# A planner that knows VectorE's pause behind a result it needs: delta-rule attention and a SwiGLU layer on one core

## The chip, the core and the metric

The kernel runs on one core of a Trainium2 chip. A core has five engines that run side by side, each through its own list of instructions in order: TensorE (PE) multiplies matrices, VectorE (DVE) and ScalarE (ACT) do elementwise work, GpSimd (POOL) does small odd jobs, and SyncE (SP) issues most DMA transfers. The metric is the device time of one execution in microseconds (us), the median of several runs.

## The reference

There are two layers in a row. The first is DeltaNet attention over 4 batches and 8 heads with 768 steps and head size 48:

```python
for t in range(S):
    kt, vt, bt = (k_n[:, :, t], v[:, :, t], beta[:, :, t, None])
    y[:, :, t] = np.einsum('bhd,bhde->bhe', q[:, :, t], state)
    v_old = np.einsum('bhde,bhd->bhe', state, kt)
    state = state + bt[:, :, :, None] * np.einsum('bhd,bhe->bhde', kt, vt - v_old)
```

Here `k_n` is `k` divided by its norm. The result, 3072 tokens of width 384, goes through an RMS norm with gain and a SwiGLU layer of width 1536: `(silu(xn @ w_gate) * (xn @ w_val)) @ w_out`. All inputs arrive in 64-bit or 32-bit floats as the reference makes them; the kernel computes in fp32.

## The kernel before

**Tiles.** The 768 steps are cut into 12 tiles (`c` from 0 to 11) of 64 steps. Inside a tile the step-by-step recurrence becomes matrix algebra. A triangular matrix of key products is inverted, and that inverse times a right-hand side gives the tile's updates `u_`. The `state` goes from tile to tile. Each tile's outputs then go through the SwiGLU layer (`ffn_plain` for tiles 0 and 1, `ffn` for tiles 2 to 11).

**The inverse.** Tiles 0 and 1 invert blocks of 16 (`prep16`), tiles 2 to 11 blocks of 32 (`invert`). The work is a chain on VectorE. After a few opening operations (L1023, L1048, L1053, L1058) come 15 steps, 7 in `prep16`. Each step is a `tensor_tensor` that multiplies into the scratch `acc` (L1070; L903 in `prep16`) and a `tensor_reduce` that adds three planes of it (L1076; L909). Each of these reads what the one in front of it wrote. Behind the last step the inverse is copied out, written to DRAM (`dx`, `dxt`) and read back by DMA in other layouts (`m1bd`, `x2bd`, `mt`). TensorE then merges it (L1124, L1152) and multiplies it with the right-hand side (L1281). After that `u_` (L1349, L1351) leads to `pu` (L1317), `ku` (L1404) and the new state.

**Weights.** The SwiGLU weights arrive as 64-bit floats in 18 pieces of 768 columns. `weights` converts each with one ScalarE operation (L619) and VectorE operations L607, L610 and L615. The last sum of the two halves is done in one of two ways: on TensorE by two products with the identity into PSUM and a ScalarE copy (L631, L632, L636) for pieces `n < NPE`, or on VectorE (L639) for the others. `NPE` is 1, so piece 0 takes the first way.

**The SwiGLU layer.** `ffn_plain` makes its products at L1558 and L1540. Before tile 2's layer, VectorE forms sums of the weights (`factors`, L1616; `out_factors`, L1687). `ffn` then uses them for a fast scheme with fewer products: for each of two halves 15 products (L1651), whose results are added up on VectorE (L1661) or copied by ScalarE (L1663), and then `down` (L1708, L1717).

**The planner.** No order of instructions is written out. Each piece of work is put into a `Plan` with `P.add(engine, duration, function, priority, r=reads, w=writes)`. One such operation may issue one or several instructions. `Plan.forward` lays the operations out in time with the given durations: of all operations that are ready, the one that can start first goes next, and the key decides between equals. On VectorE an operation may start `OVERLAP["DVE"]` = 0.08 us before the one ahead of it ends, and before the change this holds also for one that needs the other's result. `Plan.backward` turns a finished layout into new keys. `run` does that for a number of rounds, then tries the shakes of keys whose seeds stand in `MOVES`, each from where the last left off, and keeps the best order. That order is what each engine gets. Before time 70 `filler` puts spare products (L1826) where the layout leaves TensorE empty.

The diff touches `Plan.add`, `forward` and `backward`, the two `step` functions of `prep16` and `invert`, `NPE`, and the durations that several `P.add` calls are given.

Of the kernel before, what the change touches and what calls it, by code (L numbers as in the profile page):

```python
# [20 lines left out]
L = 16  # L21
# [4 lines left out]
ROUNDS, MOVES = (22, 17), (22002180, 22002182, 22003335, 22003342, 22003359, 22003366, 22003748, 22003755, 22003872, 22003889, 22003903, 22003920, 22003934, 22003951, 22003980, 22004653, 22004660, 22004729, 22004746, 22004753, 22004770, 22004784, 22004801, 22004870, 22004877, 22004894, 22004901, 22004918, 22004925, 22004932, 22004949, 22004994, 22005011, 22005221, 22008697, 22008780, 22010194, 22010220, 22010239, 22010256, 22010270, 22010287, 22010301, 22010318, 22010400, 22010466, 22010535, 22010559, 22010560, 22010566, 22010583, 22010590, 22010614, 22010676, 22010683, 22010700, 22010707, 22010714, 22010731, 22010738, 22013940, 22014280, 22014565, 22014620, 22014780, 22014860, 22015546, 22015640, 22016400, 22016640, 22019860, 22020512, 22020620, 22020980, 22021900, 22022178, 22022500, 22023240, 22023744, 22024759, 22025599, 22028580, 22432695, 22434395, 22436663, 22437300, 22438400, 22439440, 22441380, 22441780, 22442460, 22442900, 22730144, 22731520, 22731920, 22731968, 22731982, 22732667, 22734384, 22734484, 22734852, 22735265, 22735300, 22735678, 22736628, 22736790, 22736838, 22737523, 22737533, 22737829, 22738662, 22738951, 22740560, 22746034, 22747420, 22747741, 22748419, 22749152, 22749290, 22753826, 22754194, 22755471, 22755620, 22756220, 22756789, 22757140, 22758049, 22758160, 22759790, 22760680, 22762300, 22763820, 22766102, 22766200, 22767004, 22767644, 22767940, 22768119, 22769086, 22771213, 22773629, 22773808, 22776028, 22785537, 22851960, 22853134, 22856837, 22860912, 22861215, 22862065, 22863655, 22864481, 22865240, 22865320, 22866860, 22869820, 22898160, 22899809, 22901540, 22901620, 22902120, 22902927, 22906589, 22906700, 22907300, 22907540, 22908258, 22910819, 22910877, 22911445, 22912860, 22913386, 22918927, 22919082, 22919880, 22920476, 22922892, 22922909, 22923180, 22923960, 22924706, 22926702, 22926967, 22928120, 22928416, 22928557, 22929276, 22929700, 22938627, 22940028, 22940145, 22940630, 22942998, 22943731, 22944000, 22944137, 22944285, 22944574, 22944715, 22945414, 22946570, 22947417, 22947699, 22948384, 22948477, 22950700, 22951100, 22952944, 22955921, 22956334, 22957415, 22967671, 22968620, 23135508, 23135773, 23136045, 23136069, 23136100, 23136186, 23137876, 23138585, 23139731, 23139865, 23140612, 23140877, 23142006, 23142520, 23143245, 23144220, 23144460, 23144640, 23145389, 23146680, 23149200, 23149620, 23149700, 23149932, 23151911, 23153000, 23153329, 23155077, 23155490, 23157118, 23160928, 23161513, 23163940, 23166040, 23172120, 23180693, 23181278, 23181371, 23181691, 23181722, 23182283, 23182383, 23182407, 23182782, 23182803, 23183216, 23183388, 23183512, 23183653, 23183694, 23183949, 23184090, 23184107, 23186217, 23186499, 23186967, 23187091, 23188237, 23188502, 23191307, 23191751, 23194752, 23194814, 23196170, 23233009)  # L26
# [8 lines left out]
SHAKE = 0.12  # L35
SPARE = 0.5
# [35 lines left out]
class Plan:  # L72
# [48 lines left out]
    def forward(self, banks, until):  # L121
# [43 lines left out]
        while len(order) < len(self.ops):  # L165
# [78 lines left out]
    def backward(self):  # L244
# [8 lines left out]
        while left:  # L253
# [91 lines left out]
def kernel(  # L345
# [57 lines left out]
    NPE, NRAW, NCV = 1, 3, 2  # L403
# [94 lines left out]
    def setup():  # L498
# [12 lines left out]
        P.add("POOL", 1.0, lambda: make_identity(nc, ident), 0, w=["ident"])  # L511
# [22 lines left out]
        P.add("DVE", 0.9, places2, 2, r=["ident"], w=["put"])  # L534
        P.add("ACT", 1.7, lambda: nc.scalar.activation(out=rs[0], in_=mhalf, func=ACTF.Silu), -1, r=["half"], w=[("rs", 0)])
# [34 lines left out]
    def weights(n0, n1):  # L570
# [14 lines left out]
        for n, (dst, src, keys) in list(enumerate(todo))[n0:n1]:  # L585
# [33 lines left out]
            P.add("ACT", 0.84, lambda high=high, top=top: nc.scalar.activation(out=top, in_=high.bitcast(FP32), func=ACTF.Prelu, scale=2.0**-112, alpha=2.0**32), pr, r=rk, w=cak)  # L619
# [163 lines left out]
    def prep16(c):  # L783
# [113 lines left out]
        for j in range(0, L - 2, 2):  # L897
            n, m = j + 2, L - 2 - j

            def step(j=j, n=n, m=m):  # L900
# [7 lines left out]
                )  # L908
                nc.vector.tensor_reduce(  # L909
# [6 lines left out]
            P.add("DVE", 0.37 + 0.0052 * n * m, step, pi, r=ab, w=ak)  # L916
# [93 lines left out]
    def invert(c):  # L1010
# [28 lines left out]
        P.add("ACT", 0.5, start, pd, r=["half"], w=AK)  # L1039
        P.add("ACT", 0.9, start2, pd + 0.5, r=bkeys, w=AK)  # L1040
# [22 lines left out]
        P.add("DVE", 0.3, share3, pi, r=[("at", 0), ("at", 1)], w=AK)  # L1063
        P.add("DVE", 0.69, share2, pi, r=xkeys, w=[("at", 0), ("at", 1)])
        for j in range(0, W - 2, 2):
            n, m = j // 2 + 1, W - 2 - j

            def step(j=j, n=n, m=m):
# [6 lines left out]
                )  # L1075
                nc.vector.tensor_reduce(  # L1076
# [6 lines left out]
            P.add("DVE", 0.37 + 0.0052 * n * m, step, pi, r=[("at", 0), ("at", 1)], w=AK)  # L1083
# [93 lines left out]
    def recur(c):  # L1177
# [175 lines left out]
        def change(h):  # L1353
            for g_, xs in places(h):
                P.add("DVE", V(384), lambda xs=xs, g_=g_: nc.vector.tensor_tensor(out=parts(zb, h, xs), in0=found(g_), in1=parts(u_, h, xs), op=ALU.subtract), pr, r=[g_, *uk(h)], w=zk(h))
# [67 lines left out]
        for h in halves:  # L1423
# [13 lines left out]
            else:  # L1437
                for g in range(2):
# [3 lines left out]
                    ), py, r=[gy[g]], w=[("yn", p) for p in range(2)])  # L1442
                for p in range(2):

                    P.add("ACT", A(384) + 0.2, lambda p=p, gy=gy: nc.scalar.activation(
                        out=gy[p].t[:, 0:DM], in_=yn[:, p], func=ACTF.Square, scale=1.0 / math.sqrt(DM), accum_out=ms[i2][:, p, 0:1],
                    ), py, r=[("yn", p)], w=[gy[p], ("ms", i2, p)], last=gy[p])
# [9 lines left out]
            P.add("POOL", 1.1 if c else 0.7, root, py, r=["half"], w=[(k_, i2, p) for p in h for k_ in ("ms", "rs")])  # L1457
# [5 lines left out]
            else:  # L1463
                for p in range(2):
                    P.add("ACT", A(384), lambda p=p: nc.scalar.mul(yn[:, p], yn[:, p], rs[i2][:, p : p + 1]), py, r=[("rs", i2, p)], w=[("yn", p)])
            if c >= XSQ:
# [7 lines left out]
                for k_ in range(KT):  # L1474
                    P.add("ACT", A(256), lambda k_=k_: nc.scalar.mul(xf[:, 2 * k_ : 2 * k_ + 2], xf[:, 2 * k_ : 2 * k_ + 2], g_sb[:, k_ : k_ + 1]), pxv, r=["g"], w=[xkeys[0]] + ([xkeys[1]] if k_ == KT - 1 else []))  # L1475
                continue
            for p in h:
# [16 lines left out]
                for k_ in range(KT):  # L1494
                    P.add("ACT", A(128), lambda p=p, psx=psx, k_=k_: nc.scalar.mul(
                        xdst[:, 2 * k_ + p], psx.t[:, 128 * k_ : 128 * k_ + 128], g_sb[:, k_ : k_ + 1]
                    ), pxv, r=[psx, "g"], w=[xkeys[p]], last=psx)
        if c > 1:
            X = lambda a, n, step=1: xf[:, a : a + step * (n - 1) + 1 : step]
            for dst, a, b_, op, n in (  # L1500
# [11 lines left out]
                ), pxv, r=[("xp", 0)], w=["xc", ("xp", 1), ("cva", 0)])  # L1512
# [349 lines left out]
```

## Time and profile before

| what | us |
|---|---|
| median of 3 runs | 671.26 (670.19 to 671.73) |
| the profiled execution | 677.52 |
| its span, first to last instruction | 675.8 |
| TensorE busy | 657.2 (97%) |
| VectorE busy | 576.2 (85%) |
| ScalarE busy | 297.9 (44%) |
| GpSimd busy | 88.0 (13%) |

The profiled execution took 6.26 us more than the median of the runs. The profile's groups name the source line, the engine, the operation and its tiles, then the number of instructions, their busy time, the mean duration of one in ns, and the idle time in front of them with what ended it. TensorE records an fp32 product twice. Ends of TensorE records are modelled, so its busy time says less about its real load than that of other engines. A timeline row gives start and duration in us.

### The profile page before, as it was taken

The numbers are of one execution on the slowest core, as the hardware profiler recorded it, in microseconds if no ns is written. First come the engines' busy times: TensorE is split into PE (matmuls) and PEld (weight loads), VectorE is DVE, ScalarE is ACT, GpSimd is POOL, SyncE is SP. The second block draws the span as 40 slices with busy tenths as digits, with TensorE's granted clock in tenths as the row PEclk, the third lists the DMA queues.
The fourth block names the chain that finished last, engine by engine and source line by source line (L and its number), as shares of the span: only waits on it lengthen the run. The fifth ranks groups of instructions, "written<-read, shape, count | busy, mean of one in ns | idle before, by whom it ended". The sixth has DMA issues, their size and how long they took to land.

```text
span 675.8 us, 23477 instructions
## 1 busy us (share of the span) xinstructions
PE 657.2 (97%) x10052; PEld 607.2 (90%) x10052; DVE 576.2 (85%) x1200; ACT 297.9 (44%) x683; POOL 88.0 (13%) x105
## 2 busy tenths in 40 slices
PE   8898999999999999999899999999999999999997
PEld 6876777778799999999899999999999999999997
DVE  5998889999999998997899899899899699457473
ACT  7553543524336445345246336246345344343341
POOL 4113111031031030030030021030031001000000
PEclk9998999999999999999899999999999999999999
DMA  9574577636415457347447437457437434202100
GB/s 227 127 191 129 118 191 165 137 59 112 63 24 96 68 132 117 59 110 116 74 101 126 77 90 132 82 117 123 80 77 125 80 58 82 47 2 48 24 1 24
DMA packets 270430, 64.40 MB, mean 95 GB/s; under 512 B 256979, under 2 KB 262134, under 8 KB 270326
## 3 DMA queue, kind: packets, MB, share of 16 engines
q1 hardware_dynamic: 267046, 62.12, 46.5%
q8 instruction: 79, 1.29, 0.8%
q10 hardware_dynamic: 3280, 0.79, 0.6%
q14 instruction: 25, 0.20, 0.1%
HBM read 45.30 MB, written 17.56 MB: 93 GB/s over the span
## 4 chain that ended last, share of the span: by engine, by line
PE 65%; DVE 21%; SPq 5%; DMA 4%; issue 3%; ACT 1%; POOL 0%; DVEq 0%; POOLq 0%; ACTq 0%
PE bank L1651 35%; PE bank L1708 15%; SPq L487 5%; DVE acc L1076 4%; DVE acc L1070 3%; PE bank L1558 3%; PE bank L704 3%; PE bank L1199 2%; PE bank L1317 1%; DVE tmp L1661 1%; DMA at<-dkk 1%; PE bank L1540 1%; DVE more L1616 1%; DMA q<-in_q_dram 1%; DMA x2bd<-dx 1%
## 5 line engine op out<-in xcount | busy, mean ns | idle before, releaser
L1651 PE MATMUL bank<-xf,w_in 128*128 128x128 f32 x1440 | 179.2, 276 | 0.6 <-DVE tmp L1661 0.6
L1651 PEld LDWEIGHTS bank<-xf,w_in 128*128 128x128 f32 x1440 | 169.8, 192 | 1.7 <-DVE tmp L1661 0.8
L1661 DVE TENSOR_TENSOR tmp<-tmp,bank 128x512 f32<-128x512 f32 x180 | 119.8, 680 | 27.9 <-PE bank L1651 24.3
L1651 PE MATMUL bank<-xf,more 128*128 128x128 f32 x960 | 124.9, 277 | 1.8 <-DVE tmp L1661 1.8
L1651 PEld LDWEIGHTS bank<-xf,more 128*128 128x128 f32 x960 | 115.2, 192 | 4.3 <-DVE tmp L1661 3.2
L1663 ACT COPY tmp<-bank 128x512 f32<-128x512 f32 x120 | 68.1, 585 | 64.8 <-PE bank L1651 52.9
L1667 ACT ACTIVATE tmp<-tmp 128x256 f32<-128x256 f32 x120 | 49.7, 417 | 98.0 <-DVE tmp L1661 97.3
L731 POOL TENSOR_TENSOR knrm<-ksum,half 128x16 f32<-128x16 f32 x12 | 35.8, 2981 | 324.8 <-DVE ksum L730 309.5
L1076 DVE TENSOR_REDUCE acc<-acc 128x30 f32<-128x90 f32 (+4 forms) x150 | 70.9, 473 | 5.1
L1708 PE MATMUL bank<-wo_sb,hf 128*128 128x192 f32 x360 | 64.0, 328 | 0.0
L1708 PEld LDWEIGHTS bank<-wo_sb,hf 128*128 128x128 f32 x360 | 58.2, 191 | 0.7 <-ACT tmp L1713 0.2
L1070 DVE TENSOR_TENSOR acc<-acc,at 128x60 f32<-128x60 f32 (+4 forms) x150 | 52.7, 351 | 2.3
L1668 DVE TENSOR_TENSOR hf<-tmp 128x256 f32<-128x256 f32 x120 | 48.5, 420 | 6.6 <-ACT tmp L1667 5.5
L1540 PE MATMUL bank<-wo_sb,hf 128*128 128x384 f32 x96 | 35.3, 496 | 1.9 <-DVE hf L1566 1.8
L1558 PE MATMUL bank<-xf,w_in 128*128 128x256 f32 x144 | 34.8, 392 | 0.2 <-DVE hf L1566 0.2
L1558 PE MATMUL bank<-xp,w_in 128*128 128x256 f32 x144 | 33.8, 382 | 0.0
L1558 PEld LDWEIGHTS bank<-xp,w_in 128*128 128x128 f32 x144 | 26.8, 190 | 5.5 <-DVE hf L1566 0.3
L1558 PEld LDWEIGHTS bank<-xf,w_in 128*128 128x128 f32 x144 | 26.9, 192 | 4.7 <-DVE hf L1566 0.5
L1565 ACT ACTIVATE tmp<-bank 128x256 f32<-128x256 f32 x24 | 9.2, 383 | 43.7 <-PE bank L1558 36.4
L1713 ACT COPY tmp<-bank 128x192 f32<-128x192 f32 x30 | 9.5, 317 | 42.0 <-PE bank L1708 40.2
L1540 PEld LDWEIGHTS bank<-wo_sb,hf 128*128 128x128 f32 x96 | 17.3, 190 | 11.8 <-DVE hf L1566 3.7
L1510 DVE TENSOR_TENSOR xf<-xf 128x256 f32<-128x256 f32 (+1 forms) x70 | 24.0, 382 | 1.9 <-ACT xf L1475 1.1
(203 smaller groups left out, 988.6 us busy)
## 6 DMA issues: line engine op xcount, KB each, us to landing
at<-dkk SPq DMA_DIRECT2D x20, 256.0 KB, 3.8
more<-in_moe_w_gate_dram SPq DMA_DIRECT2D x6, 768.0 KB, 5.3
vt<-in_v_dram SPq DMA_DIRECT2D x24, 192.0 KB, 4.2
k<-in_k_dram SPq DMA_DIRECT2D x23, 192.0 KB, 4.3
out_dram<-tmp SPq DMA_DIRECT2D x46, 96.0 KB, 2.2
more<-in_moe_w_val_dram SPq DMA_DIRECT2D x5, 768.0 KB, 7.0
more<-in_moe_w_out_dram SPq DMA_DIRECT2D x5, 768.0 KB, 7.3
dsq<-k SPq DMA_DIRECT2D x6, 512.0 KB, 2.6
```

The costliest lines, as they stand in the source:

```text
L487: op = P.add(eng, dur + (0.08 if eng == "SP" else 0.0), lambda: queue.dma_start(out=dst, in_=src), prio, r, w, lat=0.7)
L731: P.add("POOL", 2.95, lambda: nc.gpsimd.tensor_tensor(out=knrm[i2], in0=ksum[i2], in1=half, op=ALU.pow), pn, r=[("ksum", i2), "half"], w=[ ...
L1070: nc.vector.tensor_tensor(out=acc[:, 1:3, 0:n, j + 2 : W].rearrange("p a i t -> p i a t"), in0=acc[:, old, 0:n, j : j + 2, None].to_broadc ...
L1076: nc.vector.tensor_reduce(out=acc[:, new, 0:n, j + 2 : W], in_=acc[:, lo : lo + 3, 0:n, j + 2 : W].rearrange("p a i t -> p i t a"), axis=A ...
L1540: nc.tensor.matmul(po[p].t[:, 0:DM], hf[:, spot(f), 128 * p : 128 * p + 128], wo_sb[:, spot(f)], start=(f == f0), stop=(f == f1 - 1), skip ...
L1558: nc.tensor.matmul(ps.t[:, TOK * side : TOK * side + TOK], w_in[:, side, h_, 3 * t + i_, n : n + 128], x_[:, 2 * t : 2 * t + 2].rearrange( ...
L1651: nc.tensor.matmul(g.t[:, 128 * z : 128 * z + 128], fac[:, side, 128 * f : 128 * f + 128], xf[:, xs], start=(begin and z == 0), stop=False ...
L1661: P.add("DVE", V(512), lambda t=t, g=g: nc.vector.tensor_tensor(out=t, in0=t, in1=g.t, op=ALU.add), -1, r=[g], w=[tk], last=g)
L1663: P.add("ACT", A(512), lambda t=t, g=g: nc.scalar.copy(t, g.t), -1, r=[g], w=[tk], last=g)
L1667: P.add("ACT", A(256), lambda t=t: nc.scalar.activation(out=t[:, 0:256], in_=t[:, 0:256], func=ACTF.Silu), -1, w=[tk])
L1668: P.add("DVE", V(256), lambda t=t, f0=f0, p=p: nc.vector.tensor_tensor(out=hf[:, spot(f0) : spot(f0) + 2, 128 * p : 128 * p + 128], in0=t[ ...
L1708: nc.tensor.matmul(g.t[:, 0:192], a_[:, f], b_[:, f], start=(begin and f == 0), stop=(f == 5), skip_group_check=True)
```

## The change

1. **The pause.** A constant `TIED = 0.034` is added. In `forward`, an operation that needs the result of a VectorE operation, itself on VectorE, may start only 0.034 us behind that one's end. Before, it could start 0.08 us ahead of the end. An operation with the new flag `loose=True` keeps the old rule. `backward` gets the same term. `loose` is set at four kinds of operations (L1058, L1355, L1439, L1510), which share a key with the one ahead without using its result.
2. **The steps.** Each inverse step, so far one operation of the plan with two instructions, becomes two operations, `spans` (the multiplication) and `sums_` (the reduction). The instructions themselves are the same.
3. **Durations.** The figures that the planner is given for a dozen operations are altered (identity, `places2`, the first activation, weight conversion on ScalarE, the clearing of `acc`, the square, the GpSimd root, the scaled copies).
4. **The first piece.** `NPE` goes from 1 to 0: the sum of weight piece 0 is done on VectorE (L639).
5. **The search.** `ROUNDS, MOVES` hold another seed, another number of rounds and another list: 278 seeds before, 282 after.

Since the planner works out the order anew, every engine's order differs.

```diff
-ROUNDS, MOVES = (22, 17), (
...
+ROUNDS, MOVES = (21, 13), (
...
+TIED = 0.034
...
-    def add(self, eng, dur, fn, prio, r=(), w=(), lat=0.15, ps=(), last=(), size=0):
+    def add(self, eng, dur, fn, prio, r=(), w=(), lat=0.15, ps=(), last=(), size=0, loose=False):
...
-        op.size, op.first = size, self.first
+        op.size, op.first, op.loose = size, self.first, loose
...
-                u.at = max(u.at, at[op.eng] if u.eng == op.eng and not op.dma else end + op.hop(u) + u.slack)
+                u.at = max(u.at, (end + TIED if op.eng == "DVE" and not u.loose else at[op.eng]) if u.eng == op.eng and not op.dma else end + op.hop(u) + u.slack)
...
-                gap = d.end - d.start - d.dur + (0.0 if d.eng == op.eng and not d.dma else d.hop(op) + op.slack)
+                gap = d.end - d.start - d.dur + ((TIED if d.eng == "DVE" and not op.loose else 0.0) if d.eng == op.eng and not d.dma else d.hop(op) + op.slack)
...
-    NPE, NRAW, NCV = 1, 3, 2
+    NPE, NRAW, NCV = 0, 3, 2
...
-        P.add("POOL", 1.0, lambda: make_identity(nc, ident), 0, w=["ident"])
+        P.add("POOL", 0.6, lambda: make_identity(nc, ident), 0, w=["ident"])
...
         for j in range(0, W - 2, 2):
             n, m = j // 2 + 1, W - 2 - j
 
-            def step(j=j, n=n, m=m):
+            def spans(j=j, n=n, m=m):
                 old, new, lo = (3, 0, 1) if j % 4 else (0, 3, 0)
                 nc.vector.tensor_tensor(
                     out=acc[:, 1:3, 0:n, j + 2 : W].rearrange("p a i t -> p i a t"),
...
                     op=ALU.mult,
                 )
+
+            def sums_(j=j, n=n, m=m):
+                old, new, lo = (3, 0, 1) if j % 4 else (0, 3, 0)
                 nc.vector.tensor_reduce(
                     out=acc[:, new, 0:n, j + 2 : W],
                     in_=acc[:, lo : lo + 3, 0:n, j + 2 : W].rearrange("p a i t -> p i t a"),
...
-            P.add("DVE", 0.37 + 0.0052 * n * m, step, pi, r=[("at", 0), ("at", 1)], w=AK)
+            P.add("DVE", 0.15 + 0.0021 * n * m, spans, pi, r=[("at", 0), ("at", 1)], w=AK)
+            P.add("DVE", 0.165 + 0.0034 * n * m, sums_, pi, r=[("at", 0), ("at", 1)], w=AK)
...
-        P.add("ACT", 0.5, start, pd, r=["half"], w=AK)
-        P.add("ACT", 0.9, start2, pd + 0.5, r=bkeys, w=AK)
+        P.add("ACT", 1.05, start, pd, r=["half"], w=AK)
+        P.add("ACT", 0.66, start2, pd + 0.5, r=bkeys, w=AK)
...
-        P.add("DVE", 0.3, share3, pi, r=[("at", 0), ("at", 1)], w=AK)
+        P.add("DVE", 0.3, share3, pi, r=[("at", 0), ("at", 1)], w=AK, loose=True)
...
-            P.add("POOL", 1.1 if c else 0.7, root, py, r=["half"], w=[(k_, i2, p) for p in h for k_ in ("ms", "rs")])
+            P.add("POOL", 1.1, root, py, r=["half"], w=[(k_, i2, p) for p in h for k_ in ("ms", "rs")])
...
-                    P.add("ACT", A(384), lambda p=p: nc.scalar.mul(yn[:, p], yn[:, p], rs[i2][:, p : p + 1]), py, r=[("rs", i2, p)], w=[("yn", p)])
+                    P.add("ACT", A(384) + 0.1, lambda p=p: nc.scalar.mul(yn[:, p], yn[:, p], rs[i2][:, p : p + 1]), py, r=[("rs", i2, p)], w=[("yn", p)])
```

The steps of `prep16` are split in the same way.

More of the change, by code (lines that the diff above doesn't have):

```diff
@@ L533, in setup @@
         P.add("DVE", 0.7, places, 1, r=["ident"], w=["pick"])
-        P.add("DVE", 0.9, places2, 2, r=["ident"], w=["put"])
-        P.add("ACT", 1.7, lambda: nc.scalar.activation(out=rs[0], in_=mhalf, func=ACTF.Silu), -1, r=["half"], w=[("rs", 0)])
+        P.add("DVE", 1.32, places2, 2, r=["ident"], w=["put"])
+        P.add("ACT", 0.25, lambda: nc.scalar.activation(out=rs[0], in_=mhalf, func=ACTF.Silu), -1, r=["half"], w=[("rs", 0)])
         P.add("POOL", 0.7, masks, 0, w=["mask"])
@@ L615, in s5 @@
                 nc.vector.scalar_tensor_tensor(out=cc, in0=low, scalar=by, in1=cc, op0=ALU.mult, op1=ALU.mult)
-            P.add("ACT", 0.84, lambda high=high, top=top: nc.scalar.activation(out=top, in_=high.bitcast(FP32), func=ACTF.Prelu, scale=2.0**-112, alpha=2.0**32), pr, r=rk, w=cak)
+            P.add("ACT", 0.92, lambda high=high, top=top: nc.scalar.activation(out=top, in_=high.bitcast(FP32), func=ACTF.Prelu, scale=2.0**-112, alpha=2.0**32), pr, r=rk, w=cak)
             P.add("DVE", 0.57, s2, pr, w=cak)
@@ L908, in step @@
                 )
+            def sums_(j=j, n=n, m=m):
+                old, new, lo = (3, 0, 1) if j % 4 else (0, 3, 0)
+                cols = slice(L * c + j + 2, L * c + L)
                 nc.vector.tensor_reduce(
@@ L914, in step @@
                 )
-            P.add("DVE", 0.37 + 0.0052 * n * m, step, pi, r=ab, w=ak)
+            P.add("DVE", 0.15 + 0.0021 * n * m, spans, pi, r=ab, w=ak)
+            P.add("DVE", 0.165 + 0.0034 * n * m, sums_, pi, r=ab, w=ak)
         xflat = x.rearrange("p i t -> p (i t)")
@@ L1066, in invert, with spans @@
             n, m = j // 2 + 1, W - 2 - j
-            def step(j=j, n=n, m=m):
+            def spans(j=j, n=n, m=m):
                 old, new, lo = (3, 0, 1) if j % 4 else (0, 3, 0)
@@ L1075, in step, with sums_ @@
                 )
+            def sums_(j=j, n=n, m=m):
+                old, new, lo = (3, 0, 1) if j % 4 else (0, 3, 0)
                 nc.vector.tensor_reduce(
@@ L1354, in change @@
             for g_, xs in places(h):
-                P.add("DVE", V(384), lambda xs=xs, g_=g_: nc.vector.tensor_tensor(out=parts(zb, h, xs), in0=found(g_), in1=parts(u_, h, xs), op=ALU.subtract), pr, r=[g_, *uk(h)], w=zk(h))
+                P.add("DVE", V(384), lambda xs=xs, g_=g_: nc.vector.tensor_tensor(out=parts(zb, h, xs), in0=found(g_), in1=parts(u_, h, xs), op=ALU.subtract), pr, r=[g_, *uk(h)], w=zk(h), loose=True)
         for h in halves:
@@ L1441, in recur @@
                         in1=gy[g].t[:, 0:DM].rearrange("s (y e) -> s y e", e=D), op=ALU.add,
-                    ), py, r=[gy[g]], w=[("yn", p) for p in range(2)])
+                    ), py, r=[gy[g]], w=[("yn", p) for p in range(2)], loose=True)
                 for p in range(2):
-                    P.add("ACT", A(384) + 0.2, lambda p=p, gy=gy: nc.scalar.activation(
+                    P.add("ACT", A(384), lambda p=p, gy=gy: nc.scalar.activation(
                         out=gy[p].t[:, 0:DM], in_=yn[:, p], func=ACTF.Square, scale=1.0 / math.sqrt(DM), accum_out=ms[i2][:, p, 0:1],
@@ L1474, in recur @@
                 for k_ in range(KT):
-                    P.add("ACT", A(256), lambda k_=k_: nc.scalar.mul(xf[:, 2 * k_ : 2 * k_ + 2], xf[:, 2 * k_ : 2 * k_ + 2], g_sb[:, k_ : k_ + 1]), pxv, r=["g"], w=[xkeys[0]] + ([xkeys[1]] if k_ == KT - 1 else []))
+                    P.add("ACT", A(256) + 0.09, lambda k_=k_: nc.scalar.mul(xf[:, 2 * k_ : 2 * k_ + 2], xf[:, 2 * k_ : 2 * k_ + 2], g_sb[:, k_ : k_ + 1]), pxv, r=["g"], w=[xkeys[0]] + ([xkeys[1]] if k_ == KT - 1 else []))
                 continue
@@ L1494, in recur @@
                 for k_ in range(KT):
-                    P.add("ACT", A(128), lambda p=p, psx=psx, k_=k_: nc.scalar.mul(
+                    P.add("ACT", A(128) + 0.07, lambda p=p, psx=psx, k_=k_: nc.scalar.mul(
                         xdst[:, 2 * k_ + p], psx.t[:, 128 * k_ : 128 * k_ + 128], g_sb[:, k_ : k_ + 1]
```

4 lines of the change are left out of this document (2 added, 2 removed).

## The prediction

> **What bounds the kernel now.** I read the page's totals first, then the busy time of each engine by stretch.
>
> ```profile
> span 675.8 us, 23477 instructions
> PE 657.2 (97%) x10052; PEld 607.2 (90%) x10052; DVE 576.2 (85%) x1200; ACT 297.9 (44%) x683; POOL 88.0 (13%) x105
> ```
>
> ```profile
> 0.00:20.00 20.00, 16.51 (x286) 12.45 (x286) 12.90 (x47) 14.06 (x24) 6.83 (x16) 1.00 0.86 199
> 20.00:240.00 220.00, 212.26 (x3418) 177.97 (x3419) 206.14 (x415) 98.41 (x223) 35.94 (x34) 0.99 0.54 115
> 240.00:500.00 260.00, 256.51 (x4252) 247.72 (x4252) 233.89 (x493) 116.84 (x279) 35.64 (x41) 0.99 0.55 100
> 500.00:600.00 100.00, 100.00 (x1479) 97.66 (x1479) 79.14 (x165) 43.40 (x103) 8.64 (x14) 1.00 0.40 73
> 600.00:675.80 75.80, 71.94 (x636) 71.41 (x628) 44.12 (x83) 25.19 (x58) 0.92 (x2) 1.00 0.09 22
> ```
>
> The columns after the stretch's length are PE, its weight loads, VectorE, ScalarE, GpSimd, granted clock, DMA share, GB/s. TensorE looks full everywhere, but its weight loads tell more: 97.66 of 100 us late in the run, only 177.97 of 220 between 20 and 240. There TensorE has room and VectorE, at 206.14 of 220 (94%), has hardly any. From 500 on it is the other way round. The chain of waits between 100 and 200 says the same:
>
> ```profile
> by line: DVE acc L1076 11.7%; PE bank L1558 10.7%; DVE acc L1070 8.6%; DVE more L1616 7.6%; DMA x2bd<-dx 6.9%; PE bank L1651 5.7%; SPq L487 5.7%; PE bank L1540 5.4%; issue 4.5%; DVE hf L1566 4.0%; DVE w_in L1616 3.2%; DVE tmp L1661 2.5%; DV
> ```
>
> The inverse's steps (L1070, L1076) and the weight sums (L1616) lead it. So a microsecond of VectorE is worth most before 240. Later it counts only where TensorE waits for VectorE:
>
> ```profile
> PE bank L704 <- issue: 3.0, 1, 3.0
> PE bank L1651 <- DVE tmp L1661: 2.4, 6, 0.8
> PE bank L1540 <- DVE hf L1566: 1.8, 3, 0.7
> PE bank L1199 <- issue: 1.5, 1, 1.5
> PE bank L1558 <- DVE hf L1566: 0.2, 1, 0.2
> ```
>
> **The pause and the split steps.** The timeline of VectorE inside an inverse (start, duration):
>
> ```profile
> 174.11 0.27 DVE L1070 TENSOR_TENSOR acc<-acc,at 128x112 f32<-128x112 f32 x1
> 174.42 0.35 DVE L1076 TENSOR_REDUCE acc<-acc 128x56 f32<-128x168 f32 x1
> 174.68 0.41 DVE L1566 TENSOR_TENSOR hf<-tmp,bank 128x256 f32<-128x256 f32 x1
> 175.01 0.32 DVE L1070 TENSOR_TENSOR acc<-acc,at 128x156 f32<-128x156 f32 x1
> 175.36 0.42 DVE L1076 TENSOR_REDUCE acc<-acc 128x78 f32<-128x234 f32 x1
> ```
>
> The reduction at 175.36 starts 0.03 us after its multiplication ends (175.01 + 0.32). L1566, which needs neither, starts 0.09 before the end of what is ahead of it (174.42 + 0.35 = 174.77), and the next L1070 starts 0.08 before L1566 ends. So a dependent neighbour costs 0.03 + 0.08 = 0.11 us of VectorE, and foreign work put between the two saves that. The Trainium skill, page "VectorE: DVE Perf Modes", section "The DRAIN you can't avoid", speaks against this: each VectorE operation is followed by a flush that holds the next one, whatever it waits for, and only fewer operations help. By it the saving would be 0 and the sum below 0.9 us of loss. The three starts above do not agree with it.
>
> How many such pairs go is read from the instruction orders, which tell places and no times. Dependent steps that stand side by side, old to new: in the two inverses of 16, 13 to 11 and 10 to 0 (of 13); in the ten of 32 (of 29), 22, 20, 22 to 0, 0, 3, then 145 to 113 in the last seven. In the first stretch, with the inverses of tiles 0 to 4, that is 87 to 14, so 73 × 0.11 = 8.0 us of VectorE; later 32 × 0.11 = 3.5 us.
>
> **The first piece's sum.** What it takes now, and the rows of one conversion on VectorE:
>
> ```profile
> 36.58 1.13 PE L631 MATMUL bank<-xf,ident 128*128 128x512 f32 x2
> 37.54 1.02 PE L632 MATMUL bank<-tmp,ident 128*128 128x512 f32 x2
> 38.31 0.29 DVE L1460 TENSOR_SCALAR xp<-ident,rs 128x128 f32<-128x128 f32 x1
> 38.40 1.50 PE L1485 MATMUL bank<-xp,yn 128*128 128x128 f32 x12
> ```
>
> ```profile
> L607 DVE TENSOR_SCALAR xf<-xf 128x768 uint32<-128x768 uint32 x9 | 5.0, 552 | 0.1
> L610 DVE TENSOR_SCALAR tmp<-xf 128x768 uint32<-128x768 uint32 x9 | 5.1, 566 | 0.2
> L615 DVE SCALAR_TENSOR_TENSOR tmp<-more,tmp 128x768 f32<-128x768 uint32 x8 | 7.8, 969 | 0.2
> L639 DVE TENSOR_TENSOR w_in<-xf,tmp 128x768 f32<-128x768 f32 x5 | 4.7, 933 | 0.0
> L1566 DVE TENSOR_TENSOR hf<-tmp,bank 128x256 f32<-128x256 f32 x24 | 9.8, 412 | 0.0
> L715 DVE STREAM_TRANSPOSE qt<-q 128x1024 f32<-128x1024 f32 x10 | 12.4, 1236 | 0.1
> L1246 DVE TENSOR_TENSOR r<-vt,bank 128x384 f32<-128x384 f32 x20 | 10.3, 548 | 5.7 <-PE bank L1199 5.7
> ```
>
> VectorE gets one L639 more: 0.93 less the overlap 0.08, so 0.85 us, in the full stretch. TensorE is freed of two pairs of products, the larger taking it from 36.58 to 38.40, 1.8 us. But L1485 behind them also needs the scaled identity of L1460, which starts at 38.31, and the new order has four more spare products, so PE issues as many as before. I credit 0; ends: a gain of 1.8 if all of it was on the path, a loss of 0.85 more if the sum comes late for the first L1558. ScalarE loses two copies (L636), at 44% busy no matter.
>
> **Durations, seeds and the order.** No instruction is removed by these; they decide the order. SP and POOL issue the same 603 and 110 instructions. The new figures for ScalarE and GpSimd (1.05 for the clearing of `acc`, 1.1 for the root of tile 0, and so on) issue nothing and cost nothing; they could only spare waits that I cannot name singly, so 0, between the ends that the sum's other terms already span.
>
> Three things in the new order matter. First, weights: the fifteen steps of tile 2's inverse now hold 35 foreign operations (before 13), so that 17 of the 18 conversions are done by its end, against 10 of 17. Each conversion wants its piece loaded earlier by that much:
>
> ```profile
> more<-in_moe_w_gate_dram SPq DMA_DIRECT2D x6, 768.0 KB, 5.3
> more<-in_moe_w_out_dram SPq DMA_DIRECT2D x5, 768.0 KB, 7.3
> ```
>
> A piece lands in 5.3 to 7.3 us (median from issue), three buffers take turns, and the DMA engines are busy 0.54 of the time between 20 and 240, so there is room for the earlier loads. I take 0; if a piece is late, VectorE takes the next operation in its order only after it, up to 7.3 us once. Second, the inverse of tile 2 therefore ends later, and with it its 18 transfers on SP (two `dx`, two `dxt`, two `m1bd`, four `x2bd`, eight `mt`), which now stand behind the last weight load (before, two weight loads stood between the `dxt` and the `m1bd`) but behind eight more loads of q; what that can cost is the first rival. Third, at the end: 184 products L1651 stand behind the last L1317, 180 before.
>
> ```profile
> 635.96 21.44 PE bank L1651 x192
> ```
>
> A product is two records, so 4 products are 4 × 2 × 21.44 / 192 = 0.9 us that may come late. I count this in full as a loss, though it costs nothing if that L1317 is ready earlier. The two issue stalls of PE (3.0 and 1.5 us) sit where dense small products pass; the new order may lose them or add such ones: 0, ends -4.5 and +4.5.
>
> **Sum.** First stretch 8.0 - 0.85 = 7.15 us of VectorE, passed on as far as VectorE is busy there, 94%: 6.7. Later up to 3.5, limited by PE's waits for VectorE, 2.4 + 1.8 + 0.2 = 4.4 in all, most of them short; I take 0.5. Against it 0.9. Net 6.3 us. The profiled execution would go from 677.52 to 671.2. It lies 6.26 above the median 671.26, and the same difference applied to the median gives 665.0.
>
> **Rivals.** *The inverse comes late for TensorE (slower).* Tile 2's inverse is stretched by its foreign work. Differences: L607 +5, L610 +4, L615 +4, L639 +5, L1566 +4, L1246 +1, L715 -1, which is 2.8 + 2.3 + 3.9 + 4.7 + 1.6 + 0.5 - 1.2 = 14.6, less 22 overlaps of 0.08 and 22 pauses of 0.11: 10.4 us. What hangs on it:
>
> ```profile
> 107.69 0.29 DVE L1076 TENSOR_REDUCE acc<-acc 128x30 f32<-128x90 f32 x1
> 129.71 0.65 PE L1152 MATMUL bank<-x2bd,yn 128*32 128x128 f32 x16
> ```
>
> ```profile
> 114.74 1.29 PE bank L1558 x6
> 116.03 1.29 PE bank L1540 x4
> 121.55 3.75 DMA x2bd<-dx
> ```
>
> The last reduction ends at 107.98, the last transfer lands at 125.30, L1152 starts at 129.71: 4.4 us to spare. The new order sets 142 instead of 119 plain products ahead of tile 2's L1281. At 1.29 us for three (L1558) or two (L1540) these 23 give 9.9 to 14.8 us, so the spare time becomes 4.4 - 10.4 + 9.9 to 14.8, 3.9 to 8.8. It holds, unless the transfers, queued on SP behind loads of q, take longer than the 17.3 us measured here. Each microsecond beyond is one of PE standing still, for tile 2 and again for tile 3, whose steps are spread as well. It decides from 3.15 us per tile, where the gain is eaten; at 5 each the time is 665.0 + 10 = 675.0.
>
> *TensorE bounds already before 240 (smaller gain).* Its busy column there is 212.26 of 220. Then only PE's recorded waits for VectorE can go, half of 4.4: 671.26 - 2.2 = 669.1. Against it stands the low weight-load share.
>
> *The pause is there behind any instruction (no change).* Then nothing is saved and L639 is added: 671.26 + 0.85 = 672.1.
>
> **How the numbers follow.** My forecast 48%, the small gain 18%, no change 9%, the late inverse or another worse order 25%. No change means within 0.2% (1.3 us), about what the measurement can tell. So faster 0.64 (all of the first two but a sliver), same 0.11, slower 0.25. Low end: all 11.5 of pauses less 0.85, and a 3.0 stall gone, 671.26 - 13.65 = 657.6; high end the late inverse, 675.0. The range is 657.6 to 675.0, the likeliest case's own 661 to 668.
>
> **What would show it.** Right: L639 eighteen times and no L631; VectorE rows of steps with foreign work starting before the end of the step ahead; the first L1651 and L1661 earlier than before; PE's weight loads above 178 us in 20 to 240. Wrong: waits of L1124 or L1152 for `x2bd` or `m1bd`, long issue stalls, or VectorE idle before 240 for weight pieces, which are now wanted earlier.

## The result and the profile after

The changed kernel takes 663.79 us (662.73 to 665.12) against 670.78 us for the kernel before in the same series: a ratio of 0.9895, 95% interval 0.987 to 0.9921, or 7.0 us less. A later series gave 0.989 (0.9862 to 0.9918), 7.4 us less. In it the executions with a granted clock (the share of full speed that TensorE was allowed, averaged over the execution) of 0.997 take 663.63 to 664.72 us (four) against 671.30 to 674.37 us (four), so the clock does not make the difference. The forecast was 665.0 from 671.26, 6.3 us less.

The page of the changed kernel, totals and the chain that ended last:

```profile
span 661.2 us, 23485 instructions
PE 649.0 (98%) x10052; PEld 603.5 (91%) x10052; DVE 564.4 (85%) x1201; ACT 294.9 (45%) x681; POOL 87.3 (13%) x105
PE 92%; DVE 4%; DMA 2%; issue 1%; ACT 0%; SPq 0%; ACTq 0%; DVEq 0%
```

Before, the chain was TensorE for 65% and VectorE for 21% of the span (59% and 26% in a second profile of the kernel before); now TensorE makes up 92% (89% in a second one of the changed kernel). Profiled spans must be compared with care. The profile on which the prediction rests was of a long execution: the kernel before profiled once more has a span of 668.5 us. The windows of that second profile of the kernel before:

```profile
20.00:240.00 220.00, 214.66 (x3563) 180.48 (x3558) 209.58 (x423) 98.07 (x223) 39.48 (x34) 1.00 0.53 116
240.00:500.00 260.00, 257.60 (x4170) 249.20 (x4169) 237.02 (x501) 121.09 (x288) 37.93 (x43) 1.00 0.55 102
500.00:600.00 100.00, 100.00 (x1535) 97.41 (x1534) 77.43 (x160) 42.98 (x103) 5.36 (x12) 1.00 0.38 66
```

and those of the changed kernel:

```profile
20.00:240.00 220.00, 215.66 (x3601) 185.18 (x3601) 205.91 (x433) 98.92 (x230) 38.78 (x37) 1.00 0.55 119
240.00:500.00 260.00, 259.04 (x4192) 251.48 (x4191) 238.26 (x509) 120.66 (x287) 37.17 (x44) 1.00 0.56 104
500.00:600.00 100.00, 100.00 (x1538) 97.44 (x1538) 74.63 (x152) 43.27 (x103) 4.58 (x8) 1.00 0.35 62
```

Between 20 and 240 VectorE does ten more instructions (433 against 423) in 3.7 us less busy time, and TensorE loads weights for 4.7 us more (185.18 against 180.48; 183.59 in the second profile of the changed kernel). But equal windows do not hold equal work, since the changed kernel runs ahead. So the gain is better placed by the starts of equal products. The first ones of the fast scheme, in the second profile of the kernel before and in the changed kernel (L1651 is now L1661):

```profile
178.53 1.05 PE L1651 MATMUL bank<-xf,more 128*128 128x128 f32 x8
171.16 1.16 PE L1661 MATMUL bank<-xf,more 128*128 128x128 f32 x8
```

They start 7.4 us earlier. The last L1317 (now L1327) starts 8.2 us earlier, and TensorE ends 7.3 us earlier (657.3 against 664.7). The gain is there before 180, and little is added or lost behind it.

VectorE inside tile 2's inverse, changed kernel (L1076 is now the multiplication, L1085 the reduction):

```profile
99.76 0.39 DVE L1076 TENSOR_TENSOR acc<-acc,at 128x240 f32<-128x240 f32 x1
100.08 0.54 DVE L608 TENSOR_SCALAR xf<-xf 128x768 uint32<-128x768 uint32 x1
100.55 0.55 DVE L1085 TENSOR_REDUCE acc<-acc 128x120 f32<-128x360 f32 x1
101.03 0.40 DVE L1576 TENSOR_TENSOR hf<-tmp,bank 128x256 f32<-128x256 f32 x1
101.36 0.40 DVE L1076 TENSOR_TENSOR acc<-acc,at 128x252 f32<-128x252 f32 x1
101.69 0.54 DVE L611 TENSOR_SCALAR tmp<-xf 128x768 uint32<-128x768 uint32 x1
102.16 0.58 DVE L1085 TENSOR_REDUCE acc<-acc 128x126 f32<-128x378 f32 x1
```

A foreign operation (one that is no step of the inverse) stands between any two steps of this inverse, and each operation starts 0.07 us before the end of the one ahead (100.08 against 99.76 + 0.39 = 100.15). The 0.03 us gaps of the old rows are gone here.

TensorE's recorded waits, longest first, changed kernel:

```profile
PE bank L1836 <- issue: 2.4, 1, 2.4
PE bank L686 <- DMA q<-in_q_dram: 1.5, 1, 1.5
PE bank L1836 <- POOL below L540: 1.4, 1, 1.4
PE bank L705 <- DVE kt L716: 0.8, 1, 0.8
PE bank L942 <- DVE w_in L935: 0.5, 1, 0.5
```

The waits for VectorE's L1661 and L1566 in the SwiGLU layer, 4.4 us in the first profile before and 2.7 in the second, do not appear any more. The two longest issue stalls (the profile's name for time in which an engine waits for nothing that it shows) are gone too. One of 2.4 us stands at a new place, at time 37 in front of spare products; in the second profile of the changed kernel it is 3.5 us.

### The profile page after: what moved, and what is told of

Read it like the earlier page. It is cut to its first block, busy times and chain, and to the rows that moved or that the text cites. A ratio compares the mean times of both kernels' runs of the same rounds, so it can differ in the third digit from the quotient of the medians.

```text
span 661.2 us, 23485 instructions
## 1 busy us (share of the span) xinstructions
PE 649.0 (98%) x10052; PEld 603.5 (91%) x10052; DVE 564.4 (85%) x1201; ACT 294.9 (45%) x681; POOL 87.3 (13%) x105
## 4 chain that ended last, share of the span: by engine, by line
PE 92%; DVE 4%; DMA 2%; issue 1%; ACT 0%; SPq 0%; ACTq 0%; DVEq 0%
PE bank L1661 39%; PE bank L1718 21%; PE bank L1568 10%; PE bank L1550 5%; PE bank L705 3%; PE bank L1209 3%; PE bank L1327 2%; PE bank L1291 2%; PE bank L1414 1%; DMA q<-in_q_dram 1%; PE bank L1317 1%; PE bank L1134 1%; PE bank L1162 1%; PE bank L686 1%; DMA q<-dsq 1%
## 5 line engine op out<-in xcount | busy, mean ns | idle before, releaser
L1661 PE MATMUL bank<-xf,w_in 128*128 128x128 f32 x1440 | 178.3, 276 | 0.1
L1661 PEld LDWEIGHTS bank<-xf,w_in 128*128 128x128 f32 x1440 | 169.5, 192 | 1.1 <-ACT tmp L1673 0.3
L1661 PE MATMUL bank<-xf,more 128*128 128x128 f32 x960 | 124.2, 277 | 0.0
L1661 PEld LDWEIGHTS bank<-xf,more 128*128 128x128 f32 x960 | 114.8, 192 | 1.6 <-issue 0.4
L1085 DVE TENSOR_REDUCE acc<-acc 128x30 f32<-128x90 f32 (+4 forms) x150 | 69.7, 465 | 2.0
L1076 DVE TENSOR_TENSOR acc<-acc,at 128x60 f32<-128x60 f32 (+4 forms) x150 | 53.1, 354 | 2.0
L1550 PE MATMUL bank<-wo_sb,hf 128*128 128x384 f32 x96 | 33.9, 489 | 0.0
L1106 POOL COPY acc<-acc 128x128 f32<-128x128 f32 x40 | 19.2, 511 | 76.5 <-DVE acc L1085 76.2
L1550 PEld LDWEIGHTS bank<-wo_sb,hf 128*128 128x128 f32 x96 | 17.8, 190 | 9.3 <-issue 0.2
```

The source lines that it names most:

```text
L1076: nc.vector.tensor_tensor(out=acc[:, 1:3, 0:n, j + 2 : W].rearrange("p a i t -> p i a t"), in0=acc[:, old, 0:n, j : j + 2, None].to_broadc ...
L1085: nc.vector.tensor_reduce(out=acc[:, new, 0:n, j + 2 : W], in_=acc[:, lo : lo + 3, 0:n, j + 2 : W].rearrange("p a i t -> p i t a"), axis=A ...
L1550: nc.tensor.matmul(po[p].t[:, 0:DM], hf[:, spot(f), 128 * p : 128 * p + 128], wo_sb[:, spot(f)], start=(f == f0), stop=(f == f1 - 1), skip ...
L1661: nc.tensor.matmul(g.t[:, 128 * z : 128 * z + 128], fac[:, side, 128 * f : 128 * f + 128], xf[:, xs], start=(begin and z == 0), stop=False ...
```

## The experiments

Nine kernels tell the parts of the change apart; two more runs repeat the kernel before and the changed one, and one measures the pause alone. "Pairs" are dependent inverse steps side by side in VectorE's order, in the inverses of tiles 0 to 4 and in all twelve; ratios are to the kernel before in the same series.

| kernel | pairs, tiles 0-4 | pairs, all | us | ratio (95%) |
|---|---|---|---|---|
| before, again | 87 | 232 | 670.61 | 0.9991 (0.9974 to 1.0008) |
| changed, again | 14 | 127 | 664.45 | 0.989 (0.9862 to 0.9918) |
| joined | 64 | 209 | 668.79 | 0.9957 (0.9932 to 0.9982) |
| pulled | 71 | 184 | 668.01 | 0.9949 (0.992 to 0.9979) |
| first sum | 87 | 232 | 672.4 | 0.9999 (0.9977 to 1.0022) |
| before, unsearched | 90 | 230 | 680.08 | 1.013 (1.0109 to 1.0152) |
| length, unsearched | 94 | 228 | 677.02 | 1.0078 (1.0053 to 1.0104) |
| length, pulled | 84 | 182 | 677.38 | 1.0084 (1.0057 to 1.0111) |
| changed, unsearched | 20 | 106 | 667.16 | 0.9928 (0.9896 to 0.996) |
| untied, unsearched | 98 | 242 | 695.78 | 1.036 (1.0334 to 1.0386) |
| no late filler | 14 | 127 | 665.76 | 0.9898 (0.9859 to 0.9938) |

**The pause by itself.** Additions of 128 and of 512 columns:

```diff
+        for n in (128, 512):
+            for _ in range(40):
+                add(one, n)
+            for _ in range(20):
+                add(one, n)
+                add(two, n)
```

> A kernel of additions on VectorE alone, which computes nothing of the reference: 40 additions to one tile in a row, each needing the one before; then 40 that go to two tiles in turn, so that none needs its neighbour; first 128 columns wide, then 512. Theory: start to start, a dependent addition takes 0.11 us more than one of two turns, at both widths, 4.4 us per 40. Rival, a flush behind every operation: the same time for both.

The timeline of VectorE in this kernel, first the end of the dependent row of 128 columns, then the turns:

```profile
2.39 13.29 DVE L26 TENSOR_TENSOR one<-one,y 128x128 f32<-128x128 f32 x41
15.60 0.28 DVE L26 TENSOR_TENSOR two<-two,y 128x128 f32<-128x128 f32 x1
15.80 0.28 DVE L26 TENSOR_TENSOR one<-one,y 128x128 f32<-128x128 f32 x1
16.01 0.28 DVE L26 TENSOR_TENSOR two<-two,y 128x128 f32<-128x128 f32 x1
16.21 0.28 DVE L26 TENSOR_TENSOR one<-one,y 128x128 f32<-128x128 f32 x1
16.41 0.28 DVE L26 TENSOR_TENSOR two<-two,y 128x128 f32<-128x128 f32 x1
```

In turns an addition starts every 0.20 us. The 41 of the merged row take 13.29 us, 0.32 us each. Over 39 distances from start to start the means are 0.325 and 0.202 us at 128 columns, 0.726 and 0.602 us at 512. The pause is 0.123 and 0.124 us, the same at both widths. The rule weighed in the prediction (the Trainium skill, page "VectorE: DVE Perf Modes", section "The DRAIN you can't avoid"), by which the next operation always waits for the flush, does not hold for these operations. The same section of the Trainium skill adds that a next operation that is not held starts earlier, which the prediction left out; with that the additions in turns agree, which start 0.08 us before the recorded end of the one ahead (15.80 against 15.60 + 0.28).

**Joined: the changed kernel with its pauses back.**

```diff
-        for op, s in best[1]:
+        leads = {id(op.pair) for op in self.ops if hasattr(op, "pair")}
+        seq = []
+        for op, s in best[1]:
+            if id(op) in leads:
+                continue
+            if hasattr(op, "pair"):
+                seq.append((op.pair, s))
+            seq.append((op, s))
+        for op, s in seq:
             op.start = s
```

> The changed kernel with one edit to VectorE's order: each inverse multiplication is put back right in front of its reduction, so side-by-side dependent steps go from 127 to 209 (14 to 64 in the inverses of tiles 0 to 4, 113 to 145 later). Every other engine's order stays. Theory that the pauses carry the gain: 50 x 0.11 = 5.5 us more VectorE time before 240, nearly all passed on, and a little of the later 3.5: 668 to 670 us against 663.8. Rival that the earlier weight conversions and sums carry it: under 1 us more, 664 to 665 us.

Measured 668.79 us, inside the first theory's range and outside the rival's. Against the changed kernel that is 0.9957 - 0.989 = 0.0067 of some 671 us, 4.5 us. So the order of the conversions, which stays, does not carry the gain alone. Of some 7 us, 4.5 go when 82 of the 105 pauses come back; the two intervals together leave some 2.5 us to each side, so 2.0 to 7.0. What stays in this kernel, some 3 us, has several possible causes: the 23 early pauses that remain filled (23 x 0.123 = 2.8 us), the order of the conversions, and the new durations, which no kernel here tests alone.

**Pulled: the kernel before with some of its pauses filled.** `step` is cut in two functions that are issued as before, but:

```diff
+            if not hasattr(op, "parts"):
+                foreign.append(n)
+                continue
+            if PULL and len(foreign) >= 2 and any(hasattr(d, "parts") for d in op.deps):
+                early[foreign[-1]] = op.parts[0]
+                gone.add(n)
+            foreign = []
```

> The kernel before with one edit to VectorE's order: where two or more foreign operations stand between two inverse steps, the next multiplication is pulled ahead of the last of them. Side-by-side dependent steps go from 232 to 184 (87 to 71 in the inverses of tiles 0 to 4). Theory that the pauses carry the gain: 16 x 0.11 = 1.8 us before 240 passed on and some of the later 32 x 0.11 = 3.5: 668 to 669.5 us against 670.8. Rival that the order of the weights carries it: no change, 670 to 671.5 us.

Measured 0.9949, 3.4 us less (1.4 to 5.4), with no other order touched. The median, 668.01 us, lies at the low end of the first theory's range and outside the rival's. 16 early and 32 late pauses at 0.123 are 5.9 us in all, so a good half of them was passed on. One profile of each kernel, both with full granted clock, places the gain: the first product of the fast scheme starts 0.9 us earlier (177.6 against 178.5), the last L1317 2.8 us earlier (593.0 against 595.8). So in this order late pauses count too, with some 2 of 3.9 us. The gain also speaks against another reading of joined, that any edit to a searched order costs time.

**First sum: weight piece 0 on VectorE, in the old order.**

```diff
-                    def s6(ps=ps, top=top[:, flat], cc=cc[:, flat], m=m):
-                        nc.tensor.matmul(ps.t[:, 0:m], ident, top, start=True, stop=False)
-                        nc.tensor.matmul(ps.t[:, 0:m], ident, cc, start=False, stop=True)
+                    def s6(x_=x_, dst=dst, top=tiled(top), cc=tiled(cc)):
+                        if x_ == 0:
+                            nc.vector.tensor_tensor(out=dst, in0=top, in1=cc, op=ALU.add)
...
-                    P.add("ACT", A(m), lambda dst=dst[:, cut], ps=ps, m=m, width=width: nc.scalar.copy(dst, ps.t[:, 0:m].rearrange("p (a n) -> p a n", n=width)), pr, r=[("cvp", n, x_)], w=[done[-1]], last=ps)
+                    P.add("ACT", A(m), lambda: None, pr, r=[("cvp", n, x_)], w=[done[-1]], last=ps)
```

> The kernel before, its order kept, with the sum of weight piece 0 on VectorE at the place of the first of the two products with the identity, which go, as do the two ScalarE copies. Theory (VectorE is full there): 0.85 us more, 671.6 us against 670.8. Rival that the products stood on the path to the first plain product: up to 1.8 us less, 669 us. A change under 0.5 us says that neither counts.

The ratio is 0.9999, with an interval of 1.5 us to either side: no effect seen, and neither 0.85 us of loss nor a small gain is excluded. The full 1.8 us of gain is. TensorE's waits in this kernel show one reason:

```profile
PE bank L1485 <- DVE xp L1460: 3.3, 2, 1.9
```

The products that stood behind those of piece 0 now wait for the scaled identity instead (0.2 us in the second profile of the kernel before). From 37.2 to 43.8, across the second of these waits, the granted clock in this profile is 0.50. None of the twelve executions of this kernel has a clock above 0.997, while 11 of the 29 of the kernel before beside it have 0.999 or more. So the edit also moved TensorE's gaps, and the price of the sum on VectorE alone stays open.

**The planner without its list of seeds.** Three kernels with `MOVES = ()`: the one before, the changed one, and the changed one with `TIED = -0.08`.

> The kernel before with an empty list of seeds: the planner's rounds alone. It tells what the list is worth with the old model. Theory that the model of the pause is what matters: the list fitted to a wrong model is worth little, 672 to 678 us. Rival that the search carries the gain: far above, over 680 us.

> The changed kernel with an empty list of seeds. 106 side-by-side dependent steps (kernel before without seeds: 230). Theory that the planner's knowledge carries the gain without the search: 4 to 9 us below the kernel before without seeds. Rival that the new list carries it: within 2 us of that one.

> The changed kernel with an empty list of seeds and the pause taken out of the planner (the constant set to minus the overlap), so that split steps, durations and the sum on VectorE stay. 242 side-by-side dependent steps. Theory that the pause in the model is what pulls the steps apart: 4 to 9 us above the changed kernel without seeds. Rival that the split and the durations carry it: within 2 us of it.

The kernel before without seeds took 680.08 us, above the 672 to 678 of the theory and at the edge of the rival's. Without seeds the change is worth 1.013 - 0.9928 = 0.0202, 13.6 us, nearly twice what it is worth with them and more than the 4 to 9 expected. The old list is worth 8.7 us (0.013), the new one 2.6 us (0.9928 - 0.989). So the list does not carry the gain. That the old list is worth so much contradicts the expectation: a search on a wrong model still found nearly two thirds of what the right model gives at once. The third kernel missed by far on the other side: 29.0 us above the changed kernel without seeds where 4 to 9 were expected. Its 136 more pairs explain at most 136 x 0.123 = 16.7 us. Most of the loss lies early: the first product of the fast scheme starts at 194.0 instead of 173.9. TensorE's waits in this kernel:

```profile
PE bank L1661 <- DVE tmp L1671: 6.2, 7, 1.9
PE bank L705 <- DVE qt L716: 3.9, 2, 3.5
PE bank L942 <- DVE w_in L935: 2.3, 1, 2.3
```

and its windows around the longest of them (3.5 us, until 91.2):

```profile
90.00:95.00 5.00, 2.28 (x66) 2.09 (x67) 4.90 (x11) 2.87 (x7) 3.42 (x3) 0.50 1.08 268
95.00:100.00 5.00, 3.55 (x30) 2.82 (x32) 4.72 (x14) 3.04 (x8) 1.48 (x1) 0.50 0.84 150
```

TensorE, in its fixed order, stands in front of results that are not ready, and its granted clock is down to 0.50. Over this profile the clock is at half for some 20 us (13.4 of them from 89.9 to 103.3), which costs at most 10 us; the profile of the changed kernel without seeds has no such stretch. A split step in that plan is twice 0.11 us too short, some twice the error of the kernel before, and the constant governs every other dependent pair of VectorE operations as well. How the 29.0 us divide among pauses, clock and a plan of wrong lengths was not tested for this kernel.

**The right length alone.** The kernel before without seeds, with one correction (the same in `prep16`):

```diff
-            P.add("DVE", 0.37 + 0.0052 * n * m, step, pi, r=[("at", 0), ("at", 1)], w=AK)
+            P.add("DVE", 0.463 + 0.0055 * n * m, step, pi, r=[("at", 0), ("at", 1)], w=AK)
```

> The kernel before with an empty list of seeds and one correction: an inverse step, still one operation of the plan, is given 0.463 + 0.0055 n m instead of 0.37 + 0.0052 n m, so that two steps in a row take in the plan what the two split operations with their pauses take in the changed kernel. 228 side-by-side dependent steps (230 without the correction). Theory A, that a planner which knows how long the inverse takes places TensorE's work better: well below the 680.1 us of the kernel before without seeds, 668 to 674 us. Theory B, that the filled pauses carry the gain: 678 to 680 us.

> The same, and in VectorE's order the next multiplication is pulled ahead of the last of two or more foreign operations between steps: 182 side-by-side dependent steps instead of 228 (94 to 84 in the inverses of tiles 0 to 4). At 0.123 us a pause, as measured by itself, that is 1.2 us before 240 and 4.4 later. If both theories hold in part: 1 to 3 us below the run with the length alone; theory A alone: no change; theory B alone: 3 to 5 us below.

677.02 us lies between the theories, close to the second: the right length is worth 0.0052, 3.5 us, out of 13.6. Pulling on top of it brought nothing (1.0084 against 1.0078, some 2.5 us to each side), where 1 to 3 us were expected from both together; the 3 to 5 us of theory B alone are excluded. In its order only 10 of the 46 pauses that went lie in tiles 0 to 4, which are worth 1.2 us, within the interval. The 36 late ones, 4.4 us, brought nothing that can be seen, while in the pulled kernel some 2 of 3.9 us were passed on. Whether the two orders differ in this stays open. Of the 13.6 us some 10 are left to the split steps, the filled pauses and the other new durations together.

**Both kernels again, and the late spare products.**

> The kernel before once more, unchanged, for a second profile. The profiled execution on which the prediction rests took 677.52 us, 6.26 above the median. If that excess was of this execution alone, the second profile comes out near 671 and the pieces that differ (above all the issue stalls of PE, 3.0 us at 51 and 1.5 us at 329) are smaller; if profiling always adds it, near 677 again.

> The changed kernel once more, beside the others on the same chip: 663 to 666 us, about 7 us below the kernel before.

The second profile of the kernel before took 670.32 us, at its median: the excess of 6.26 us was of the first execution alone. An issue stall at the same product (L704 at 51) is 1.0 us instead of 3.0; the one of 1.5 us at L1199 is there again. The granted clock makes up most of the rest. In the first profile it is 0.50 from 55.2 to 58.4 and from 331.7 to 334.9, each time just behind one of these two stalls; in the second it is 1.00 from 5 to 666. The same twelve records in the first profile and in the second:

```profile
331.30 3.90 PE L1708 MATMUL bank<-wo_sb,xp 128*128 128x192 f32 x12
326.53 2.22 PE L1708 MATMUL bank<-wo_sb,xp 128*128 128x192 f32 x12
```

At half clock they take 3.90 us instead of 2.22. So one such stretch costs some 1.7 us, and two of them with the 2.0 us of longer stall make 5.4 of the 7.3 us between the two spans. The stall of 1.5 us at L1199 is followed by half clock in the first profile and not in the second, so the length of the gap alone does not decide it.

```diff
-                if s < until:
+                if s < until and not 30.0 < s:
                     filler(fillers(pe, s))
```

> The changed kernel without the five spare products of TensorE behind time 30 of the plan. In the changed kernel's profile they stand at 37.0 to 38.5 and 40.9 to 41.8, right in front of products of the first tile that the rest waits for, behind an issue stall of 2.4 us. If the spare products only fill a wait for other engines: no change, 663 to 665 us. If they hold up the products behind them or feed the stall: 1 to 3 us less, 661 to 663 us. If the shift of the later instructions meets a new stall: 1 to 2 us more.

The first wait of TensorE in this kernel and its first plain product:

```profile
PE bank L1495 <- DVE acc L891: 2.4, 1, 2.4
```

```profile
40.08 2.18 PE L1568 MATMUL bank<-xf,w_in 128*128 128x256 f32 x9 [0.74 <-DVE xf L1499]
```

In the profile the plain products start at 40.08 instead of 41.84 and the span is 658.4 us. But the times (660.11 to 668.18) and the ratio 0.9898 cannot be told from the changed kernel's. The times follow the granted clock: 660.11 us at 1.000, 663.22 at 0.997, 664.25 to 668.18 in the four executions at 0.991 or 0.992, while the ten of the changed kernel in both series have 0.995 to 0.999 (662.73 to 666.51 us). So without these spare products an execution can be shorter, but the clock fell further in four of six. Whether the spare products prevent that, six executions do not show. No version tried beats the changed kernel clearly.

## Why the prediction was right

- **VectorE binds up to 240.** Right as to the place: 7.4 us are gained by the first product of the fast scheme, at 171.2. Joined, which only puts VectorE time back, loses time with TensorE's order unchanged.
- **The pause, 0.11 us.** Slightly low: 0.123 us by itself. The 73 early pauses are then 9.0 us of VectorE instead of 8.0.
- **Passed on at 94%, and 0.5 us of the late ones.** In the pair of profiles with full clock, 7.4 us are gained early (the sum had 6.7, the first piece's 0.85 already taken off) and 0.8 us more up to the last L1317 (0.5). How much of it the pauses carry is known less well. Joined gave back 4.5 us for 50 early and 32 late pauses. If the late ones count for nothing, that is 4.5 / (50 x 0.123) = 73%, and 73 early pauses carry 73 x 0.123 x 0.73 = 6.6 us; the interval of 2.0 to 7.0 us allows a third as well as all. Pulled shows late pauses that count, so 0.5 us of 3.5 was probably too small. That the sum of 6.3 us came so close to 7.0 may in part be luck: a pause too small and late pauses too cheap pull one way, a share that is perhaps too large the other.
- **First piece's sum, 0.85 us of loss.** Not seen, not excluded (0 within 1.5 us), and mixed with the clock in the kernel that tried it.
- **Four more products at the end, 0.9 us.** The stretch from the start of the last L1317 row (L1327 in the changed kernel) to TensorE's end is 69.74 us (587.60 to 657.34) against 68.85 (595.82 to 664.67) in the second profile of the kernel before: 0.9 us longer, as priced. Since that product comes 8.2 us earlier, the net is a gain.
- **The planner's part.** The sum priced what the order showed and left out why it looked so. The runs without seeds show that the pause in the model pulls the steps apart (106 pairs against 242) and that correcting a step's length alone is worth 3.5 us there.
- **The late inverse.** Did not happen. In the changed kernel's timeline the last reduction of tile 2 ends at 117.30 and L1152, now L1162, starts at 135.13:

```profile
117.04 0.26 DVE L1085 TENSOR_REDUCE acc<-acc 128x30 f32<-128x90 f32 x1
128.03 0.49 SPq L488 DMA_DIRECT2D x2bd<-dx  x1
135.13 0.64 PE L1162 MATMUL bank<-x2bd,yn 128*32 128x128 f32 x16
```

  In the first profile of the kernel before, the issues of the four `x2bd`:

```profile
120.56 4.92 SPq L487 DMA_DIRECT2D x2bd<-dx  x4
```

  The distance from reduction to product is 17.8 us, less than the 21.7 of before. The last `x2bd` is issued 10.7 us behind the reduction; before, the four took from 12.6 to 17.5 us behind it. No weight load stands between any more. TensorE's list of waits does not hold this product. The steps of this inverse take 27.5 us instead of 18.9, so 8.6 us more and not 10.4: the trace has 31 foreign operations among them, not 35, because the list of differences left out two L1522 and two L765 that are there before and not after.
- **Signs named.** L639 (now L640) stands eighteen times (the last ends at 121.2; in the second profile of the kernel before at 140.1), and the first L1651 starts at 171.2 (178.5). Weight loads between 20 and 240 are 185 us, above the 178 named, but the kernel before has 180 itself in its second profile, so this sign tells little. One sign of being wrong came: a long issue stall, 2.4 us at the spare products. It did not eat the gain.

## What to carry to other kernels

When two engines run in fixed orders side by side, look for the stretch where the fuller one binds, and count there how often an operation stands right behind the one whose result it needs: each such pair had a fixed price here (0.123 us), and a foreign operation between them saves it. Give a planner the pause and operations small enough to be pulled apart. A search on top can hide part of a wrong model, so compare models without the search as well. Look at the granted clock of each execution before reading differences of 1%.

## What was not expected

The pause does not grow with the operation: 0.123 us at 128 columns, 0.124 at 512. A planner without the pause, which takes a split inverse step for some 0.23 us shorter than it is, gave an order 29.0 us slower, more than all pauses that the order adds; 20 of them were lost by 194 us, and stretches of half clock are part of it. And the kernel's profiled execution can lie 6 to 7 us above another one of the same kernel, for the most part by a longer stall and two stretches of half clock, so differences of single profiles under 1% of the span say little without a second one.
